# Ten attention units inside the matmul blocks of a fused kernel: one tabulated slot for every step, and B's copy on Scalar

## The chip, the cores and the metric

The kernel runs on one core of one Trainium2 chip. Its engines are PE (TensorE, the matmuls; its weight loads are shown as PEld), DVE (VectorE), ACT or Scalar (ScalarE), POOL (GpSimd) and SP (SyncE, which here only issues DMAs). Each engine works through its own queue of instructions in order and waits on semaphores for the others. The metric is the device time of one execution in microseconds (us), smaller is better; the median of three runs is 579.62 us.

## The reference, cut to what matters

Three layers follow each other; only the first mixes tokens.

```python
# x (4, 8, 768, 32), a (4, 8, 768), B and C (4, 8, 768, 16); chunks along the sequence
log_a = np.log(np.clip(a, 1e-06, 1.0))
for c in range(nc):                                  # a linear recurrence, chunk by chunk
    cum = np.cumsum(la, axis=-1)
    L = np.exp(cum[..., :, None] - cum[..., None, :]) * causal
    y_intra = (C B^T * L) @ x                        # inside the chunk
    y_inter = (C @ state) * np.exp(cum)[..., None]   # from the state before
    state = np.exp(sum(la)) * state + sum_j B_j x_j exp(cum_last - cum_j)
# y as 3072 tokens x 256 features
h = ((y @ w1) * (y @ w2)) @ w3                       # 256 -> 1024 -> 1024
x2 = h @ w_out                                       # 1024 -> 256
out = np.maximum(x2 @ w_in, 0) ** 2 @ w_out2         # 256 -> 2048 -> 256
```

## The kernel before, in words

**Blocks.** The 3072 tokens are cut into seven blocks f, four of 384 tokens and three of 512 (`FBS`). A block has a first stage of 8 steps m (`ph_a`): `a_mm` makes y @ w1 and y @ w2 for 128 of the 1024 columns, Scalar copies one result out of PSUM (`asb`), DVE multiplies (`pr`), Scalar and DVE split the product into a high and a low part (`s3h`, `s3l`), and three steps later `ff_x2` multiplies with w3 @ w_out, which is made once. Then Scalar and DVE split the 256 sums (`x2h`, `x2l`). The second stage has 16 steps (`ph_h`): `ff_h1` (6 matmuls), relu on Scalar (`r`), the square on POOL (`q`), Scalar's high part `s3h` and DVE's low part `s3l`, and, three steps later (`LAG`), `ff_o` (6 matmuls). Every product is taken as three matmuls, high x high, low x high, high x low (`mm3`, L195), for precision. For the first three steps of the second stage there is no `ff_o` yet, so these slots are short on PE (3 matmuls each, after 9 that go ahead of them). The last three `ff_o` of a block (`o_tail`) run in the first two slots of the next block; at block 4 they all run in its first slot, where the pool of 384-token tiles is replaced by one of 512 (`widen`).

**Units.** The attention layer is 16 units u: a pair of units (2j, 2j+1) is the two halves of the features of 384 tokens. The steps of one unit are:

- `u_decay` (DVE, four scans, L357): the running products of the decays, from `la`, loaded by DMA;
- `u_lw` (DVE, one short product, L369) and `u_bt` (L259): a copy of B from `bs`, loaded by DMA, to `bt`, on POOL;
- `u_bd` and `u_w2` (POOL, L375 and L386): B and the state's factors with the decays;
- `u_turn` (PE): `u_cb` (C with B, 32 small matmuls into `ub`, L445), `u_gain` (what the chunk adds to the state, L396) and, for the unit before, `u_y` (L464);
- `u_x` (Scalar) and `u_xl` (DVE): the outcome of the unit before, split into `xt` or `big`, which the first stage of a block reads; `u_loads`, the DMAs of the next unit on SP (`la`, `xa`, and for an even unit four parts each of C and B);
- `u_state` (DVE, four steps, L410), four masks `u_m` (DVE, L456: `ub` times the decays), `u_carry` (Scalar, four copies, L421).

`ub` is one PSUM tile, so a turn waits until the masks of the unit before are done.

**What sets the order.** Units 0 to 5 and blocks 0 and 1 are issued by a list of numbers (`ORDER`, run by `Plan`). From block 2 on the order is that of the code: each step m of a block is a slot, counted from 0 at block 2 (block 2: first stage 0 to 7, second 8 to 23; block 3: 24 to 31 and 32 to 47; block 4: 48 to 55 and 56 to 71; block 5: 72 to 79 and 80 to 95; block 6 from 96). In each slot `run_fill` issues what `place` has put there, behind the slot's `s3h` and in front of its `s3l`, and in front of its `ff_x2` or `ff_o`. The table `TURN` says where: before, a row of seven numbers for a unit, the slots of its six first pieces (four scans; `u_lw` with `u_bt`; `u_bd` with `u_w2`) and of its turn, while the eight pieces from the turn on stand at fixed distances of 0, 0, 1, 1, 2, 2, 3 and 3 slots behind it. The names in the order below are the program's: `la<-la,cs` a scan, `la<-ub,la` a mask, `st` a state step, `la<-la` the short product, `xtl` and `big` the outcome.

Of the kernel before, what the change touches and what calls it, by code (L numbers as in the profile page):

```python
# [102 lines left out]


TURN = {
# [4 lines left out]
}  # L110


# [26 lines left out]
def mixer_kernel(ctx, tc, a, bct, xb, cst, *rest):  # L139
# [117 lines left out]
    def u_bt(u, eng="POOL"):  # L257
        copy = nc.scalar.copy if eng == "ACT" else on[eng].tensor_copy
        copy(bt[u % 2][:, :, 0:T], bs[:, u % 2, :].rearrange("p (c i) -> p c i", i=T))  # L259
# [91 lines left out]
    def u_decay(u, h):  # L351

        if h == 0 and u >= ROWS:
            un[u] = raw[u]
        la = un[u]["la"][:, h * LH:(h + 1) * LH]
        src = rows.pop((u, h))[0:TA, :] if u < ROWS else la
        nc.vector.tensor_tensor_scan(la[:, 0:TB], src[:, 0:TB], cs, 0.0, ALU.mult, ALU.add)  # L357
        if u < ROWS:
            nc.vector.tensor_tensor(
                la[:, TB:], src[:, TB:LH],  # L360
                la[:, 0:TB].rearrange("p (c i) -> p c i", i=T)[:, :, T - 1], op=ALU.mult,
            )

    def u_lw(u):

        la = un[u]["la"].rearrange("p (h i) -> p h i", i=LH)
        if u >= ROWS:
            last = la[:, :, 0:TB].rearrange("p h (c i) -> p h c i", i=T)[:, :, :, T - 1]
            nc.vector.tensor_tensor(la[:, :, TB:], la[:, :, TB:], last, op=ALU.mult)  # L369

    def u_bd(u):

        d = un[u]
        lw = d["la"].rearrange("p (h i) -> p h i", i=LH)[:, :, TB:]
        nc.gpsimd.tensor_tensor(  # L375
            bd[u % 2][:, 0:HC * N].rearrange("p (h c n) -> p h c n", h=HG, n=N),
            d["xa"][0:T, HC * D:].rearrange("p (h c n) -> p h c n", h=HG, n=N),
            lw[0:T].unsqueeze(3).to_broadcast([T, HG, NCH, N]),
            op=ALU.mult,
        )  # L380

    def u_w2(u, eng="POOL"):
        lw = un[u]["la"].rearrange("p (h i) -> p h i", i=LH)[:, :, TB:]
        copy = nc.scalar.copy if eng == "ACT" else on[eng].tensor_copy
        for h in range(HG):
            copy(w2s[u % 2][32 * h:32 * h + N, :], lw[T:TA, h, :])  # L386
# [16 lines left out]
    def u_state(u):  # L403

        d = un[u]
        s = st[u % 2]
        c0 = NCH * ((u // 2) % 2)
        g = d.get("g") or [d["yu"][:, TB + c * D:TB + (c + 1) * D] for c in range(NCH)]
        for c in range(NCH):
            nc.vector.scalar_tensor_tensor(  # L410
                s[:, c0 + c + 1, :], s[:, c0 + c, :], w2s[u % 2][:, c:c + 1],
                g[c], ALU.mult, ALU.add,
            )

    def u_carry(u):

        d = un[u]
        s = st[u % 2]
        c0 = NCH * ((u // 2) % 2)
        for h in range(HG):  # L420
            nc.scalar.copy(  # L421
                d["xa"][T:TA, h * NCH * D:(h + 1) * NCH * D].rearrange("p (c d) -> p c d", d=D),
                s[32 * h:32 * h + N, c0:c0 + NCH, :],
            )
# [27 lines left out]
    def u_m(u, h):  # L452

        d = un[u]
        s = d["la"][:, h * LH:h * LH + TB]
        nc.vector.tensor_tensor(s, d.pop(("cb", h))[0:TA, :], s, op=ALU.mult)  # L456
# [14 lines left out]
    def u_x(u):  # L471

        d = un[u]
        d["x"] = []
        j, g = divmod(u, 2)
        i0 = 0
        while i0 < TB:
            f = max(f for f in range(NF) if F0[f] <= j * TB + i0)
            i1 = min(F0[f] + FBS[f] - j * TB, TB)
            if i0 % T or i1 - i0 < T:  # L480
                i1 = min(i1, i0 - i0 % T + T)
                src = d["y"][:, i0 // T, i0 % T:i0 % T + i1 - i0]
            else:
                i1 -= i1 % T
                src = d["y"][:, i0 // T:i1 // T, :]
            if f not in xt:
                if f < WIDE:
                    xt[f] = [sb.tile([128, KD, FB], F32R, tag=f"xt{p}", name=f"xt{p}", bufs=2) for p in "hl"]
                else:
                    if f == WIDE:  # L490
                        big.append(late.tile([128, NRL, KD, FBL], F32R, tag="rawl", name="big"))
                    xt[f] = [big[0][:, 2 * (f % 2) + i] for i in range(2)]
            at0 = j * TB + i0 - F0[f]
            hi, lo = (t[:, g, at0:at0 + i1 - i0] for t in xt[f])
            if len(src.shape) == 3:
                hi, lo = (t.rearrange("p (c i) -> p c i", i=T) for t in (hi, lo))
            nc.scalar.copy(hi, src)
            d["x"].append((lo, src, hi))
            i0 = i1

    def u_xl(u):
        raw.pop(u)
        for lo, src, hi in un.pop(u)["x"]:
            nc.vector.tensor_tensor(lo, src, f32(hi), op=ALU.subtract)

    def u_loads(u):
        if EARLY + 2 <= u < NU:
            load_la(u)
            load_xa(u)
            if u % 2 == 0:  # L510
                for h in range(HG):
                    load_ct(u // 2, h)
                    load_bt(u // 2, h)

    def u_turn(u):
        if u < NU:
            u_cb(u)
            u_gain(u)
        if u > EARLY:
            u_y(u - 1)  # L520

    def u_first(u):
        return [
            *(lambda h=h: u_decay(u, h) for h in range(HG)),
            lambda: (u_lw(u), u_bt(u)),
            lambda: (u_bd(u), u_w2(u)),
        ]

    def u_then(u):
        steps = [  # L530
            lambda: u_turn(u),
            lambda: (u > EARLY and u_x(u - 1), u_loads(u + 1)),
            lambda: u > EARLY and u_xl(u - 1),
            lambda: u_state(u),
            lambda: u_m(u, 2),
            lambda: u_m(u, 3),
            lambda: (u_carry(u), u_m(u, 0)),
            lambda: u_m(u, 1),
        ]
        return steps if u < NU else steps[:3]  # L540
# [294 lines left out]
    def place(i, f):  # L835
        fill.setdefault(PLANNED * (M1 + M2) + i, []).append(f)

    for u in range(EARLY, NU + 1):
        if u < NU:
            for i, f in zip(TURN[u], u_first(u)):  # L840
                place(i, f)
        for i, f in zip((0, 0, 1, 1, 2, 2, 3, 3), u_then(u)):
            place(TURN[u][-1] + i, f)

    def ph_a(f, tail):
        for m in range(M1):
# [126 lines left out]
```

## Time and profile before

| | |
|---|---|
| median of 3 runs | 579.62 us (578.86 to 580.37) |
| profiled execution: its own time, and its span | 579.46 us, 577.5 us |
| PE / PEld busy | 559.3 us (97%) / 492.9 us (85%) |
| DVE / Scalar / POOL busy | 335.8 (58%) / 280.7 (49%) / 140.4 us (24%) |
| chain that ended last | PE 87%, DMA 4%, DVE 3%, Scalar 2% |
| HBM read and written | 39.55 MB and 3.25 MB |

The span goes from the first to the last instruction; the execution's own time has the start and the end around it. The loads of weights fill the first 100 us; from 190 us on, where block 2 and the table begin, the core moves little data. PE is the engine that is nearly always busy. Its busy time is that of modelled ends: matmuls are pipelined, and one is shown for longer than the distance to the next. So the time that PE loses is read from its waits and from the distance of starts, not from the busy share.

### The profile page before, as it was taken

The numbers are of one execution on the slowest core, as the hardware profiler recorded it, in microseconds if no ns is written. First come the engines' busy times: TensorE is split into PE (matmuls) and PEld (weight loads), VectorE is DVE, ScalarE is ACT, GpSimd is POOL, SyncE is SP. The second block draws the span as 40 slices with busy tenths as digits, with TensorE's granted clock in tenths as the row PEclk, the third lists the DMA queues.
The fourth block names the chain that finished last, engine by engine and source line by source line (L and its number), as shares of the span: only waits on it lengthen the run. The fifth ranks groups of instructions, "written<-read, shape, count | busy, mean of one in ns | idle before, by whom it ended". The sixth has DMA issues, their size and how long they took to land.

```text
span 577.5 us, 10665 instructions
## 1 busy us (share of the span) xinstructions
PE 559.3 (97%) x4182; PEld 492.9 (85%) x4182; DVE 335.8 (58%) x603; ACT 280.7 (49%) x571; POOL 140.4 (24%) x194
## 2 busy tenths in 40 slices
PE   7898999999999999999989999999999999999997
PEld 5777999999999988999979978788888778888885
DVE  6789899993655555774687454394244532232421
ACT  3678778853455334543354342454432454333543
POOL 3133223010000104641145400353200533000532
PEclk8899999999999998999999999999999999999999
DMA  7998958100120002124203200122000000000000
GB/s 230 380 330 276 294 186 211 43 1 28 53 83 19 28 1 72 25 71 116 57 22 97 71 28 0 49 49 70 1 37 1 1 1 1 36 1 0 1 1 38
DMA packets 16891, 43.49 MB, mean 75 GB/s; under 512 B 2712, under 2 KB 6024, under 8 KB 16840
## 3 DMA queue, kind: packets, MB, share of 16 engines
q1 hardware_dynamic: 16552, 42.58, 24.1%
q8 instruction: 33, 0.54, 0.4%
q10 hardware_dynamic: 288, 0.22, 0.2%
q14 instruction: 18, 0.15, 0.1%
HBM read 39.55 MB, written 3.25 MB: 74 GB/s over the span
## 4 chain that ended last, share of the span: by engine, by line
PE 87%; DMA 4%; DVE 3%; ACT 2%; issue 1%; POOL 1%; SPq 0%; POOLq 0%; ACTq 0%; DVEq 0%
PE pw L195 44%; PE acc L195 34%; PE acc L658 3%; DMA rawe<-in_w3t 3%; DMA rawl<-in_wo 2%; PE ub L445 1%; PE ub L464 1%; DVE la L357 1%; PE ub L396 1%; PE yu L464 1%; PE pacc L195 1%; ACT r L612 1%; PE cb L445 1%; ACT xa L421 0%; DVE pr L570 0%
## 5 line engine op out<-in xcount | busy, mean ns | idle before, releaser
L620 POOL TENSOR_TENSOR q<-r 128x512 f32<-128x512 f32 (+1 forms) x81 | 85.0, 1052 | 248.9 <-ACT r L612 219.8
L627 DVE TENSOR_TENSOR s3l<-q,s3h 128x384 fp32r<-128x384 f32 (+1 forms) x112 | 75.8, 686 | 101.3 <-POOL q L620 90.9
L195 PE MATMUL acc<-s3h,wo 128*128 128x384 f32 (+1 forms) x448 | 126.4, 363 | 0.0
L612 ACT ACTIVATE r<-pw 128x384 f32<-128x384 f32 (+1 forms) x107 | 56.9, 534 | 95.1 <-PE pw L195 89.5
L195 PEld LDWEIGHTS acc<-s3h,wo 128*128 128x128 f32 x448 | 82.6, 189 | 9.1 <-issue 0.3
L195 PE MATMUL acc<-s3l,wo 128*128 128x384 f32 (+1 forms) x224 | 81.2, 363 | 1.0 <-DVE s3l L627 1.0
L570 DVE TENSOR_TENSOR pr<-pw,asb 128x384 f32<-128x384 f32 (+1 forms) x56 | 34.3, 613 | 74.4 <-PE pw L195 67.4
L195 PE MATMUL pw<-x2l,wih 128*128 128x384 f32 (+1 forms) x214 | 76.8, 363 | 0.0
L624 ACT ACTIVATE s3h<-r 128x384 fp32r<-128x384 f32 (+1 forms) x112 | 63.7, 570 | 10.8 <-PE acc L195 7.7
L580 ACT CAST s3h<-pr 128x512 fp32r<-128x512 f32 (+1 forms) x47 | 26.7, 569 | 65.3 <-DVE pr L570 61.7
L566 ACT COPY asb<-pw 128x384 f32<-128x384 f32 (+1 forms) x56 | 29.3, 525 | 50.2 <-PE pw L195 42.4
L357 DVE TENSOR_TENSOR_SCAN la<-la,cs 112x384 f32<-112x384 f32 x48 | 53.2, 1138 | 0.0
L195 PEld LDWEIGHTS acc<-s3l,wo 128*128 128x128 f32 x224 | 42.3, 189 | 5.4 <-DVE s3l L627 1.3
L195 PEld LDWEIGHTS pw<-x2l,wih 128*128 128x128 f32 x214 | 40.3, 188 | 4.4 <-DVE x2l L599 0.2
L195 PE MATMUL pw<-x2h,wih 128*128 128x384 f32 x124 | 42.3, 341 | 0.0
L195 PE MATMUL pw<-x2h,wil 128*128 128x384 f32 x124 | 42.0, 339 | 0.0
L583 DVE TENSOR_TENSOR s3l<-pr,s3h 128x384 fp32r<-128x384 f32 (+1 forms) x52 | 32.1, 620 | 15.9 <-ACT s3h L580 15.6
L195 PE MATMUL acc<-s3l,wch 128*128 128x384 f32 (+1 forms) x104 | 37.9, 365 | 1.3 <-DVE s3l L583 1.3
L195 PE MATMUL acc<-s3h,wch 128*128 128x384 f32 (+1 forms) x104 | 38.2, 367 | 0.0
L195 PE MATMUL acc<-s3h,wcl 128*128 128x384 f32 (+1 forms) x104 | 37.8, 364 | 0.0
L195 PE MATMUL pw<-big,wih 128*128 128x512 f32 x90 | 36.0, 400 | 0.0
L658 PE MATMUL acc<-wo1v,ve 128*128 128x256 f32 x128 | 32.1, 402 | 3.8 <-DVE ve L315 2.9
(146 smaller groups left out, 1048.7 us busy)
## 6 DMA issues: line engine op xcount, KB each, us to landing
la<-az SPq DMA_DIRECT2D x12, 679.0 KB, 4.9
xa<-in_xb SPq DMA_DIRECT2D x16, 288.0 KB, 5.8
rawe<-in_w3t SPq DMA_DIRECT2D x9, 512.0 KB, 9.1
rawl<-in_wo SPq DMA_DIRECT2D x7, 512.0 KB, 7.4
rawl<-in_w3t SPq DMA_DIRECT2D x7, 512.0 KB, 9.2
rawe<-in_wo SPq DMA_DIRECT2D x5, 512.0 KB, 7.3
rawl<-in_w SPq DMA_DIRECT2D x5, 512.0 KB, 8.2
rawl<-in_w_in SPq DMA_DIRECT2D x5, 512.0 KB, 5.4
```

The source lines that it names most:

```text
L195: nc.tensor.matmul(ps, lhsT=w[i == 1], rhs=x[i == 2], start=first and i == 0, stop=last and i == 2)
L357: nc.vector.tensor_tensor_scan(la[:, 0:TB], src[:, 0:TB], cs, 0.0, ALU.mult, ALU.add)
L445: nc.tensor.matmul(d["cb", h][0:TA, c * T:(c + 1) * T], lhsT=bt[u % 2][r, c, :], rhs=d["ct"][r, c * T:(c + 1) * T], start=True, stop=True,)
L566: nc.scalar.copy(ab[m], ab.pop((m, 0)))
L570: nc.vector.tensor_tensor(pr, ab.pop((m, 1)), ab[m], op=ALU.mult)
L580: (nc.scalar.copy if eng == "ACT" else on[eng].tensor_copy)(pt[f, m][0], ab[m])
L583: nc.vector.tensor_tensor(pt[f, m][1], ab.pop(m), f32(pt[f, m][0]), op=ALU.subtract)
L612: nc.scalar.activation(hr[m], hp.pop(m), AF.Relu)
L620: on[eng].tensor_tensor(q, hr[m], hr[m], op=ALU.mult)
L624: nc.scalar.activation(qt[f, m][0], hr[m], AF.Square)
L627: nc.vector.tensor_tensor(qt[f, m][1], hr.pop((m, 0)), f32(qt[f, m][0]), op=ALU.subtract)
L658: nc.tensor.matmul(wps[f][j // 2][:, (j % 2) * DM:(j % 2 + 1) * DM], lhsT=t[:, j * 128:(j + 1) * 128], rhs=wo1v[:, k, :].bitcast(F32), sta ...
```

## The change

`TURN` has two tuples for a unit: six slots for the first pieces and eight for the pieces from the turn on, so that each has a slot of its own (for unit 16, which only finishes unit 15, three). The numbers come from a search over a small schedule. `u_bt` of these ten units is called with "ACT": B's copy runs on Scalar.

```diff
 TURN = {
-    6: (0, 0, 1, 1, 2, 2, 4), 7: (7, 7, 8, 8, 9, 9, 11), 8: (14, 14, 15, 16, 16, 17, 19),
...
+    6: ((1, 5, 5, 6, 6, 6), (8, 9, 9, 9, 9, 10, 10, 10)),
+    7: ((2, 3, 3, 4, 7, 8), (13, 13, 13, 13, 14, 14, 17, 18)),
...
     def u_first(u):
         return [
             *(lambda h=h: u_decay(u, h) for h in range(HG)),
-            lambda: (u_lw(u), u_bt(u)),
+            lambda: (u_lw(u), u_bt(u, "ACT")),
             lambda: (u_bd(u), u_w2(u)),
         ]
...
     for u in range(EARLY, NU + 1):
         if u < NU:
-            for i, f in zip(TURN[u], u_first(u)):
+            for i, f in zip(TURN[u][0], u_first(u)):
                 place(i, f)
-        for i, f in zip((0, 0, 1, 1, 2, 2, 3, 3), u_then(u)):
-            place(TURN[u][-1] + i, f)
+        for i, f in zip(TURN[u][1], u_then(u)):
+            place(i, f)
```

The turns stood in slots 4, 11, 19, 26, 31, 38, 46, 58, 66, 82 and (unit 16) 89; they stand now in 8, 13, 20, 25, 31, 39, 46, 57, 70, 80 and 93. Lines of the changed kernel from `TURN` on have numbers that are higher by 7.

DVE before, from slot 6 of block 2 to the start of its second stage (`pr` and `s3l` are the first stage's, `x2l` ends it, `s3l<-q` is the second stage's):

```order
L570 TENSOR_TENSOR pr<-pw,asb 128x384
L456 TENSOR_TENSOR la<-ub,la 112x384 x2
L583 TENSOR_TENSOR s3l<-pr,s3h 128x384
L570 TENSOR_TENSOR pr<-pw,asb 128x384
L456 TENSOR_TENSOR la<-ub,la 112x384 x2
L357 SCALAR_TENSOR_TENSOR la<-la,cs 112x384 x2
L583 TENSOR_TENSOR s3l<-pr,s3h 128x384
L599 TENSOR_TENSOR x2l<-acc,x2h 128x384 x2
L357 SCALAR_TENSOR_TENSOR la<-la,cs 112x384 x2
L627 TENSOR_TENSOR s3l<-q,s3h 128x384
```

DVE now, from slot 5 to the start of the second stage:

```order
L577 TENSOR_TENSOR pr<-pw,asb 128x384
L364 SCALAR_TENSOR_TENSOR la<-la,cs 112x384 x2
L590 TENSOR_TENSOR s3l<-pr,s3h 128x384
L577 TENSOR_TENSOR pr<-pw,asb 128x384
L364 SCALAR_TENSOR_TENSOR la<-la,cs 112x384
L376 TENSOR_TENSOR la<-la 112x4x4
L590 TENSOR_TENSOR s3l<-pr,s3h 128x384
L577 TENSOR_TENSOR pr<-pw,asb 128x384
L376 TENSOR_TENSOR la<-la 112x4x4
L590 TENSOR_TENSOR s3l<-pr,s3h 128x384
L606 TENSOR_TENSOR x2l<-acc,x2h 128x384 x2
L634 TENSOR_TENSOR s3l<-q,s3h 128x384
```

Unit 7's first two scans stood between the last `pr` and the last `s3l` of the first stage; now all eight scans of units 6 and 7 are done by slot 6, and the masks of unit 6 come in the second stage.

POOL before, the steps of units 6 to 8 (`bt`, `bd`, `w2s`) and the squares of block 2:

```order
L375 TENSOR_TENSOR bd_100<-xa,la 96x256
L386 COPY w2s_102<-la 16x4 x4
L620 TENSOR_TENSOR q<-r 128x384 x2
L259 COPY bt_107<-bs 128x4x96
L375 TENSOR_TENSOR bd_101<-xa,la 96x256
L386 COPY w2s_103<-la 16x4 x4
L620 TENSOR_TENSOR q<-r 128x384 x7
L259 COPY bt_106<-bs 128x4x96
```

Scalar now, where units 6 and 7 have their copies of B (slots 6 and 7 and the three first relus of the second stage):

```order
L266 COPY bt_106<-bs 128x4x96
L573 COPY asb<-pw 128x384
L587 CAST s3h<-pr 128x384
L266 COPY bt_107<-bs 128x4x96
L603 CAST x2h<-acc 128x384 x2
L619 ACTIVATE r<-pw 128x384
L631 ACTIVATE s3h<-r 128x384
L619 ACTIVATE r<-pw 128x384
L631 ACTIVATE s3h<-r 128x384
L619 ACTIVATE r<-pacc 128x384
```

`bt` of unit 7 stood behind two squares on POOL; now it stands on Scalar behind the last `s3h` of the first stage, five slots ahead of the turn of its unit.

DVE before, from the end of block 3's first stage (units 10 and 11):

```order
L599 TENSOR_TENSOR x2l<-acc,x2h 128x384 x2
L504 TENSOR_TENSOR big<-ub,big 128x384
L410 SCALAR_TENSOR_TENSOR st_104<-st_104,w2s_102,ub 128x32 x4
L627 TENSOR_TENSOR s3l<-q,s3h 128x384
L456 TENSOR_TENSOR la<-ub,la 112x384 x2
L627 TENSOR_TENSOR s3l<-q,s3h 128x384
L456 TENSOR_TENSOR la<-ub,la 112x384 x2
L357 SCALAR_TENSOR_TENSOR la<-la,cs 112x384 x2
L627 TENSOR_TENSOR s3l<-q,s3h 128x384
L357 SCALAR_TENSOR_TENSOR la<-la,cs 112x384 x2
L627 TENSOR_TENSOR s3l<-q,s3h 128x384
L369 TENSOR_TENSOR la<-la 112x4x4
```

DVE now, from the same place:

```order
L606 TENSOR_TENSOR x2l<-acc,x2h 128x384 x2
L364 SCALAR_TENSOR_TENSOR la<-la,cs 112x384 x2
L634 TENSOR_TENSOR s3l<-q,s3h 128x384
L417 SCALAR_TENSOR_TENSOR st_104<-st_104,w2s_102,ub 128x32 x4
L634 TENSOR_TENSOR s3l<-q,s3h 128x384 x2
L463 TENSOR_TENSOR la<-ub,la 112x384
L364 SCALAR_TENSOR_TENSOR la<-la,cs 112x384 x2
L376 TENSOR_TENSOR la<-la 112x4x4
L634 TENSOR_TENSOR s3l<-q,s3h 128x384
```

The four scans of unit 11 stood two and two behind the four masks of unit 10; now two stand in front of the first `s3l` of the second stage and two behind the first mask, and the other three masks follow them.

## Rows read from the trace of the kernel before

**Rows 1.** The page: engines' busy time; PE's granted clock in 40 slices

```profile
PE 559.3 (97%) x4182; PEld 492.9 (85%) x4182; DVE 335.8 (58%) x603; ACT 280.7 (49%) x571; POOL 140.4 (24%) x194
...
PEclk8899999999999998999999999999999999999999
```

**Rows 2.** Who PE waited for from 190 us on: us in total, times, longest

```profile
PE ub L445 <- POOL bt L259: 2.3, 2, 1.2
PE acc L195 <- DVE s3l L583: 1.3, 1, 1.3
PE pw L195 <- ACT asb L566: 1.2, 2, 0.7
PE acc L195 <- DVE s3l L627: 1.0, 1, 1.0
PE pw L195 <- DVE pr L570: 0.4, 2, 0.3
```

**Rows 3.** PE in time, end of block 2's first stage: start, us, what

```profile
216.70 0.44 PE L195 MATMUL acc<-s3l,wch 128*128 128x384 f32 x1 [1.34 <-DVE s3l L583]
216.99 0.34 PE L195 MATMUL acc<-s3h,wch 128*128 128x384 f32 x1
```

**Rows 4.** The chain behind the turns of units 7 and 8: start, us

```profile
225.59 0.91 PE ub L464 x32
226.50 2.22 PE acc L195 x6
228.72 1.41 PE pw L195 x6
...
246.32 0.70 PE ub L464 x32
247.03 1.24 PE acc L195 x6
248.27 1.06 PE pw L195 x6
```

**Rows 5.** Behind unit 7's turn: busy time by engine, PEclk, DMA

```profile
226.00:229.00 3.00, 3.00 (x23) 2.72 (x13) 2.15 (x4) 0.48 (x1) 1.60 (x2) 0.50 0.53 177
```

**Rows 6.** DVE in order of time, slot 7 of block 2

```profile
214.40 1.80 DVE L357 TENSOR_TENSOR_SCAN la<-la,cs 112x384 f32<-112x384 f32 x2
```

**Rows 7.** B's copy by engine: duration in ns, least/median/most

```profile
L259 POOL COPY bt<-bs x15: 498/505/1681, 7.6 to 411.1; 128x384 f32<-128x384 f32 x15
...
L259 ACT COPY bt<-bs x1: 511/511/511, 7.6 to 7.6; 128x384 f32<-128x384 f32 x1
```

**Rows 8.** POOL in order of time, ahead of unit 11's turn

```profile
301.02 1.68 POOL L259 COPY bt<-bs 128x384 f32<-128x384 f32 x1
```

**Rows 9.** SP's DMA issues behind unit 11's turn, first and last: start, us

```profile
304.98 0.31 SPq L235 DMA_DIRECT2D la<-az  x1
...
313.01 0.31 SPq L255 DMA_DIRECT2D bs<-in_bct  x1
```

**Rows 10.** Time to landing of the DMAs into la, then of those into bs

```profile
DMA to landing us min/median/max: 4.4/4.9/6.3
...
DMA to landing us min/median/max: 1.8/5.1/6.2
```

**Rows 11.** Scalar in order of time, block 4's second slot

```profile
338.60 1.22 ACT L421 COPY xa<-st 16x128 f32<-16x128 f32 x4
```

**Rows 12.** DVE's groups by form from 225 us on: xcount, busy us, mean ns

```profile
L357 DVE TENSOR_TENSOR_SCAN la<-la,cs 112x384 f32<-112x384 f32 x32 | 37.2, 1188 | 0.0
...
L456 DVE TENSOR_TENSOR la<-ub,la 112x384 f32<-112x384 f32 x36 | 18.3, 549 | 0.0
...
L410 DVE SCALAR_TENSOR_TENSOR st<-st,w2s,ub 128x32 f32<-128x32 f32 x36 | 8.8, 245 | 1.0
```

**Rows 13.** The page's groups of the square and the low part

```profile
L620 POOL TENSOR_TENSOR q<-r 128x512 f32<-128x512 f32 (+1 forms) x81 | 85.0, 1052 | 248.9 <-ACT r L612 219.8
L627 DVE TENSOR_TENSOR s3l<-q,s3h 128x384 fp32r<-128x384 f32 (+1 forms) x112 | 75.8, 686 | 101.3 <-POOL q L620 90.9
```

12 rows, old and new, of the table TURN are left out of this document.

## The prediction

> **What bounds the kernel now.** I read the page first, then PE's waits, then the places of these waits in time. The page has PE busy for 97% of the span [rows 1], so only what makes PE wait, or slows it, can move the end. From 190 us on, where the tabulated units begin, PE's waits are few [rows 2]: 2.3 us in two waits for B's copy on POOL (`bt`), 1.3 and 1.0 us for `s3l` of DVE, 0.4 us in two pieces for `pr` of DVE, and 1.2 us in two pieces for `asb` of Scalar. All are within two slots of a step of a unit. Nothing else there is idle on PE, and the matmuls themselves are the same before and after, so the change can give back these waits, what hangs on them, and no more.
>
> A wait costs more than its row says. Matmuls are shown longer than their spacing: one takes 0.34 us at 216.99 [rows 3], while six of them pass in 1.06 us [rows 4], 0.18 us apart, so each idle time starts 0.16 us late in the rows.
>
> The Trainium skill says the same in general (Trainium Kernel Development and Optimization, Performance Expectations): busy time of the matmul row is a bad measure, since matmuls are pipelined. By the idle column alone the waits below would be 5.5 us; by the spacing they are 6.6 us, and the trace is on the side of the page.
>
> One wait has a second price. After PE waited for unit 7's `bt` its granted clock is 0.50, the 1.2 GHz level, from 226 to 229 us [rows 5]. The same work after the turns of unit 7 and unit 8 [rows 4] takes 0.91 against 0.70, 2.22 against 1.24 and 1.41 against 1.06 us: 0.2 + 1.0 + 0.35 = 1.5 us lost. Behind the other turns the page's clock line stays at its highest digit [rows 1].
>
> **The change, part by part.** PE's instructions are the same in number; ten groups of them (a unit's turn) stand elsewhere. Nothing before slot 0 of block 2 (about 189 us) moves.
>
> *Scans away from the last slot of a first stage.* Before, unit 7's first two scans stand at 214.40 between `pr` and `s3l` of slot 7 [rows 6], 1.80 us, and PE, which needs this `s3l` at once, waits 1.34 us at 216.70 [rows 3]. In the new order only a short product stands there, while DVE would wait for Scalar's `s3h` anyway: that wait (1.3) goes. The two 0.4 us pieces for `pr` come from two scans in each of slots 0 and 1; now slot 0 has none and slots 1 and 2 have one each: they go. The 1.0 us for `s3l` is unit 11's four scans in slots 34 and 35, right behind unit 10's masks; now they are in 32 and 35, with the state and masks spread over 33 to 36: it goes, with little to spare (below).
>
> *B's copy to Scalar.* On POOL it takes 0.50 us alone [rows 7] but 1.68 at 301.02, beside DVE's scans [rows 8], and stands behind squares in the order; both `bt` waits of PE (2.3) are this. On Scalar the one row there is takes 0.51 us [rows 7]. Ten copies are 5.1 us on an engine that is busy for 49% of the span, and they stand two to seven slots ahead of their turns, so none is on the path. The bounds of one copy are 0.5 and, if Scalar suffered as POOL did, 1.7 us; even that is less than a slot (12 x 0.18 = 2.1 us in the second stage), of which, at 49% busy, Scalar's own operations take about half. I take 0.5, hidden. POOL keeps the `bd` and `w2` steps and its squares, which loses it nothing.
> The copy adds a wait to Scalar: for B's load. SP starts a pair's loads when the turn ends; before, it issued unit 12's decays at 304.98 and the last B part at 313.01 [rows 9], which lands at least 1.8 us later [rows 10], so 9.8 us after the turn. In the new table unit 12's copy stands four slots behind its load; eight sixes of matmuls (8.5 us) and Scalar's two operations of a slot (about 1 us) bring it there after 9.5 us, so it waits some 0.3 us, with the next relu behind it. PE needs that relu only when its PSUM buffer is taken again, one slot and a half later (18 matmuls, 3.2 us, of which the relu itself takes about a sixth): a wait of up to 2 us is hidden. For units 8 and 10 it is five and four slots (the four are long ones), for 14 ten.
>
> *The state's copies.* Unit 12's four copies `xa<-st` take 1.22 us on Scalar at 338.60 [rows 11], ahead of the next `asb`, in a slot of block 4 without `x2` matmuls; that is the shorter `asb` wait (1.2 - 0.7 = 0.5). They move to slot 54, a full slot: it goes. The other, 0.7 us, is at slot 48, where the wide pool replaces the narrow one and `asb` waits for the old tiles' last matmul. Nothing of that changes: it stays.
>
> *What is packed closer.* Three scans now share a slot (units 8, 12, 14), and units 9, 11, 12 and 13 scan one or two slots after their decays are loaded. A scan takes 1.19 us on average, a mask 0.55, a state step 0.25 [rows 12]. Three scans and an `s3l` (0.69 [rows 13]) are 4.3 us in a slot of 2.1, 2.2 late; `s3l` is used three slots on, 6.3 us, of which relu, the square (1.05 [rows 13]) and `s3l` itself need some 2.4, so about 4 us may be lost before PE notices. The tightest stretch is the start of block 3's second stage (slots 32 to 38). From `x2l` to unit 11's turn DVE has 4 scans (4.75), a state (1.0), 4 masks (2.2), 5 `s3l` (3.4): 11.4 us. PE has 9 + 48 + 6 matmuls of 0.177, 11.1 us, and starts some 0.5 later: 11.6. At the border of blocks 2 and 3 (slots 21 to 23) the same count leaves DVE 0.4 us ahead of PE. Decays land 4.4 to 6.3 us after issue [rows 10]; unit 12's scans, two slots behind the turn, come up after two sixes of matmuls and the 2.4 us of the chain to `s3l`, 4.1 us after the issue (0.2 of it passes before), so DVE loses 0.3 to 2.2 there, and PE, by the 4 us above and the masks in front of the turn in slot 46, nothing to 0.4. For all of this I add 0.2 us; the bounds are 0 and, if two of the tight places miss by as much as the waits of before did (1.2 each) and the clock falls once (1.5), 3.9.
>
> The output store of block 2 moves behind unit 10's ten loads on SP. Its `o` tile shares a buffer with `pr`, but in the new program only the `pr` of slot 31 waits for that store, some 17 us on; no cost.
>
> **The sum.** Idle 2.3 + 1.3 + 1.0 + 0.4 + 0.5 = 5.5; seven waits x 0.16 = 1.1; clock 1.5; less 0.2: 7.9 us. The profiled execution took 579.46, so 571.6; the median of the runs is 0.16 above it, so 571.7.
>
> **Rivals.**
> *The waits move.* DVE's work is not less, only spread otherwise, and two stretches have under 0.5 us in hand. For it: the sums of 11.4 and 11.6, and means that hide longer scans beside POOL. Against: `bt` no longer disturbs there, and alone a scan is near 0.9 (two in 1.80). Two waits of 1.2 and a fall of the clock: 571.7 + 3.9 = 575.6, spread from 573.5 to 577.5.
> *The clock falls without a wait.* The turn's narrow matmuls, not the wait, may have done it; then a fall stays somewhere: 573.2. Against: nine turns without a drop, one of them (unit 11's) behind a wait of 1.1. It lies inside the forecast's range.
> By the Trainium skill (TensorE: Matmul & The Clock Gate, Why this matters for your kernels) the fall belongs to idle gaps longer than any in these rows; by that rule the 1.5 would not hang on the wait, as in this rival; the one fall in the trace stands behind the longest wait but one.
> *The change does not do what it says.* Scalar's copy, in order behind relu, `s3h` and a load, is as late as POOL's was, and the turns wait as before; with the spread scans 3 us are won, with a late Scalar two of them are lost again behind Scalar: within 0.3%, about 578.5. Against: the copies stand two slots or more ahead.
> *Slower: scans wait for their load.* DVE is in order; a scan that waits for its decays holds up `s3l`, `pr` and the masks of the turn. Six units (8, 9, 10, 11, 12, 13) now scan about when the landing is due, 4 to 6 us after the turn. While it lands by 6.3 us, PE's share is small; from about 7.5 us on each of the six costs PE 1.4 and more, and the gain of 7.9 is gone. At 8 us it is 6 x 1.8 = 10.8: 582. For it: the loads compete with B's and C's. Against: 6.3 is the longest of eight.
>
> **How the numbers follow.** Forecast 0.62 (own range 570.5 to 573.4), waits move 0.20, the clock 0.05, not as said 0.06, slower 0.07. A run of this kernel tells 0.3% (1.7 us) from no change, so faster means under 577.9: 0.62 + 0.20 + 0.05 = 0.87; same 0.06; slower 0.07. The range leaves out 0.15 at the top; below 569.9 there would have to be a gain besides the waits.
>
> **What would show it.** No PE wait for `bt` in the waits; no `s3l` wait of 1 us in slots 7 and 35; PE clock 1.00 from 190 us to the end; the wait for `asb` at slot 48 still there; Scalar idle before some `bt` for the load without a PE wait behind it. Wrong would be PE waits for masks, `s3l` or `pr` at slots 24 to 26, 35 to 39 or 46, or DVE's scans waiting more than 2 us for `la`.

## The result, and the profile after

The changed kernel took 569.38 us as a median of four runs (569.02 to 570.82), the kernel before 579.24 us in the same comparison (four runs): a ratio of 0.983, 95% interval 0.981 to 0.986. Five later runs of the changed kernel gave 569.69 beside 578.66 for before, ratio 0.984 (0.981 to 0.986). The direction and the mechanism came as predicted. The time, 571.7 predicted, was 2.3 us too high, and 569.38 lies 1.1 us below the forecast's own range (570.5 to 573.4) and 0.5 us below 569.9, under which the prediction expected nothing.

The page of the changed kernel, profiled at 569.02 us; the lines answer to [rows 1], the columns of the first are busy time, share of the span and instructions:

```profile
span 567.1 us, 10661 instructions
PE 555.2 (98%) x4182; PEld 491.4 (87%) x4182; DVE 330.1 (58%) x603; ACT 285.8 (50%) x581; POOL 134.4 (24%) x184
...
PEclk8999999999999999999999999999999999999999
```

PE's busy time fell by 4.1 us (559.3 to 555.2) while the span fell by 10.4. The busy share, 97% before and 98% now, says next to nothing of that.

All that PE waited for from 186 us to the end (columns: engine, output and line, releaser; us in total, times, longest), where before there were five groups [rows 2]:

```profile
PE pw L202 <- ACT asb L573: 0.7, 1, 0.7
```

Only the `asb` wait of slot 48 is left, the one that the prediction said would stay. No new wait came in its place. The clock behind unit 7's turn, now from 222.8 to 225.1 us, in stretches of the changed kernel (columns: stretch, its length, busy time of PE, PEld, DVE, ACT and POOL with instructions, then granted clock, DMA share, GB/s), beside 0.50 in [rows 5]:

```profile
222.00:226.00 4.00, 4.00 (x108) 3.51 (x107) 1.74 (x4) 2.04 (x5) 2.11 (x2) 1.00 0.02 4
226.00:232.00 6.00, 6.00 (x36) 6.00 (x35) 4.99 (x11) 2.20 (x5) 2.26 (x2) 1.00 0.97 215
```

And the chain behind that turn (start, length, matmuls), to be read beside [rows 4]:

```profile
224.47 0.70 PE ub L471 x32
225.17 1.27 PE acc L202 x6
226.44 1.06 PE pw L202 x6
227.50 1.06 PE acc L202 x6
```

The sixes that took 2.22 and 1.41 us behind the wait of before are at 1.27 and 1.06 now. B's copy, by engine and form (shortest, median and longest in ns), and what the queue of Scalar did just ahead of it:

```profile
L266 ACT COPY bt<-bs x10: 495/502/515, 206.8 to 417.2; 128x384 f32<-128x384 f32 x10
L266 ACTq EVENT_SEMAPHORE  x9: 17/17/38, 206.4 to 386.6; - x9
```

All ten take 0.50 us, where POOL's went up to 1.68 [rows 7], and none waits for B's load: the 0.3 us that the prediction gave to unit 12's copy did not come.

DVE now waits for decays, which it never did from block 2 on before. The total, and the longest of the four in its place (DVE's timeline; idle time and releaser in brackets):

```profile
DVE la L364 <- DMA la<-az: 5.2, 4, 3.2
```

```profile
315.63 0.75 DVE L511 TENSOR_TENSOR big<-ub,big 128x96 fp32r<-128x96 f32 x4 [0.42 <-ACT big L504]
319.56 0.96 DVE L364 TENSOR_TENSOR_SCAN la<-la,cs 112x384 f32<-112x384 f32 x1 [3.17 <-DMA la<-az]
320.43 0.53 DVE L634 TENSOR_TENSOR s3l<-q,s3h 128x384 fp32r<-128x384 f32 x1
```

That is unit 13's scan in slot 47. DVE stands for 3.2 us, `s3l` behind it stands late with it, and PE has no wait there, since it uses this `s3l` only in the next block's first slot.

**Where the time went.** The start of each block can be read from PE's first matmul of it. From block 2's start to the last instruction the profiles show 388.45 us before (189.09 to 577.54) and 379.48 after (187.60 to 567.08): 8.97 less, of which 5.35 in block 2, 2.35 in block 3, 1.00 in block 4, 0.26 in block 5. Another 1.49 us lies ahead of block 2, where both run the same program.

### The profile page after: what moved, and what is told of

It reads as the page before. It is cut to its first block, busy times and chain, and to the rows that moved or that the text cites. A ratio compares the mean times of both kernels' runs of the same rounds, so it can differ in the third digit from the quotient of the medians.

```text
span 567.1 us, 10661 instructions
## 1 busy us (share of the span) xinstructions
PE 555.2 (98%) x4182; PEld 491.4 (87%) x4182; DVE 330.1 (58%) x603; ACT 285.8 (50%) x581; POOL 134.4 (24%) x184
## 4 chain that ended last, share of the span: by engine, by line
PE 92%; DMA 4%; DVE 2%; ACT 1%; issue 0%; ACTq 0%; SPq 0%
PE pw L202 47%; PE acc L202 36%; PE acc L665 2%; DMA rawe<-in_w3t 2%; PE ub L452 2%; DMA rawl<-in_w3t 2%; PE ub L471 1%; PE pacc L202 1%; PE acc L712 1%; PE cb L452 1%; PE ub L403 1%; DVE la L364 1%; PE yu L471 1%; DMA cs<-in_cst 1%; PE rows L351 0%
## 5 line engine op out<-in xcount | busy, mean ns | idle before, releaser
L634 DVE TENSOR_TENSOR s3l<-q,s3h 128x384 fp32r<-128x384 f32 (+1 forms) x112 | 73.1, 662 | 91.0 <-POOL q L627 80.8
L631 ACT ACTIVATE s3h<-r 128x384 fp32r<-128x384 f32 (+1 forms) x112 | 63.7, 570 | 10.8 <-PE acc L202 7.7
L382 POOL TENSOR_TENSOR bd<-xa,la 96x256 f32<-96x256 f32 x16 | 12.5, 783 | 180.5 <-DVE la L376 171.0
L364 DVE TENSOR_TENSOR_SCAN la<-la,cs 112x384 f32<-112x384 f32 x48 | 50.4, 1081 | 5.2 <-DMA la<-az 5.2
```

The lines of the kernel that those rows point to most:

```text
L382: nc.gpsimd.tensor_tensor(bd[u % 2][:, 0:HC * N].rearrange("p (h c n) -> p h c n", h=HG, n=N), d["xa"][0:T, HC * D:].rearrange("p (h c n) ...
L631: nc.scalar.activation(qt[f, m][0], hr[m], AF.Square)
L634: nc.vector.tensor_tensor(qt[f, m][1], hr.pop((m, 0)), f32(qt[f, m][0]), op=ALU.subtract)
```

## The experiments

In all diffs the kernel named is the base. "To the end" is the time from block 2's first matmul to the last instruction, in the profiled execution.

**The kernel before once more** (no edit).

> The kernel before, unchanged, to see what comes and goes without any change. Theory: the profiled run of before had a fall of PE's clock to 1.2 GHz in its first 40 us that the run of the changed kernel had not; block 2 then began at 189.1 instead of 187.6 us, though no instruction ahead of it is moved. If that is chance, the runs here show mean clocks of both kinds, 0.991 and about 0.994, times 1 to 2 us apart, and a median within 0.3% of before. Rival: the early 1.5 us belongs to the change; then every run of before has it (0.991, block 2 at 189.1).

It took 578.22 us (576.83 to 579.22, 12 runs), ratio 0.9995 (0.998 to 1.001). Its profile has the same five groups of waits, the clock at 0.86 from 220 to 232 us as in the first profile, and 388.57 us to the end (388.45 in the first). The mean clocks of its 12 runs lie between 0.991 and 1.000, so not every run of before has the early 1.5 us of the rival. The part that the table orders repeats within 0.2 us, while the runs of one program lie up to 4.6 us apart (576.1 to 580.7 over 48 runs of before).

**Scalar's copy alone**, in the kernel before:

```diff
-            lambda: (u_lw(u), u_bt(u)),
+            lambda: (u_lw(u), u_bt(u, "ACT")),
```

> The old table, with B's copy of the ten later units on Scalar. Theory: both waits of PE for that copy go (2.3 and 2 x 0.16), the fall of the clock behind the first one with them (1.5 to 1.7), and the two waits of 0.2 for bd in front of units 13 and 15, since POOL has less in front of it: 4.1 to 4.7 us faster, block 2 to the end 388.5 to 384 us. The waits for s3l (1.3 and 1.0), pr (0.4) and asb (0.7 and 0.5) stay. Rival (the turn's narrow matmuls make the clock fall): the clock is at 1.2 GHz for about 3.4 us behind unit 7's turn without a wait, gain 2.6 to 3. Rival (Scalar is as late as POOL was): waits for bt of 1 us stay, no gain.

577.02 us (575.68 to 579.23, 12 runs), ratio 0.997 (0.995 to 0.998): faster by 1.8 us, well under what was expected. PE's waits from 186 us on:

```profile
PE pw L195 <- ACT asb L566: 1.6, 3, 0.7
PE acc L195 <- DVE s3l L583: 1.3, 1, 1.3
PE ub L396 <- POOL bd L375: 1.2, 2, 0.8
PE acc L195 <- DVE s3l L627: 1.0, 1, 1.0
PE ub L445 <- ACT bt L259: 0.4, 1, 0.4
PE pw L195 <- DVE pr L570: 0.4, 2, 0.3
```

The 2.3 us of `bt` on POOL are gone and 1.2 us of `bd` stand in their place, in the same two turns, with 0.4 of `bt` on Scalar and 0.4 more for `asb`. `bd` was behind `bt` in POOL's order, and it has a second thing to wait for, the short product on DVE. POOL at units 7 and 11 (start, length; idle time and releaser in brackets):

```profile
222.95 0.89 POOL L375 TENSOR_TENSOR bd<-xa,la 96x256 f32<-96x256 f32 x1 [0.18 <-DVE la L369]
...
300.53 0.81 POOL L375 TENSOR_TENSOR bd<-xa,la 96x256 f32<-96x256 f32 x1 [1.49 <-DVE la L369]
```

At unit 11 that product (300.22 us) stood behind scans that ran until 299.85 and an `s3l`; at unit 7 (222.01 us) it stood behind an `s3l` that had waited for a square. B's copy itself reads no scan; on Scalar unit 7's stood behind two relus and two `s3h`. So unit 7's turn went only from 3.82 us (0.2 of it the lower clock) to 3.27, unit 11's from 3.50 to 3.21, against 2.33 without a wait. The 0.2 of `bd` at units 13 and 15, which were to go, stayed. The clock did not fall in this profile (1.00 from 220 us on), which is most of the 1.8.

**The table alone**, in the kernel after:

```diff
-            lambda: (u_lw(u), u_bt(u, "ACT")),
+            lambda: (u_lw(u), u_bt(u)),
```

> The new table, with B's copy on POOL as before. Theory: the waits for bt came from the place behind squares, two slots ahead of the turn, and the new table has the copy four to ten slots ahead; so nearly all of the gain stays: block 2 to the end 379.5 to 380.5 us against 388.5 before and 379.5 with the whole change. Rival: the copy has to leave POOL; one or two waits for bt of about 1.2 us come back, with or without a fall of the clock, 381 to 384 us.

569.89 us (569.19 to 570.4, 5 runs), ratio 0.985 (0.983 to 0.987); 379.73 us to the end, 0.25 more than in the first profile of after. PE's one wait is the `asb` of 0.7, every turn takes 2.33 to 2.39 us, and DVE's waits for `la` came to 7.8 us at no cost. Of the change's two parts the table does all that can be measured. The copy stands two to six slots ahead of its turn in the new table, not four to ten as expected, but at units 7 and 11, where PE had waited, it is six and four where it was two: POOL's copies start at 209.84 and 290.83 us there, and PE's turns need them at 223.50 and 296.36. What Scalar takes over is hidden either way.

**Scans still earlier**, in the kernel after, all four of a unit in one slot (units 8 to 13; two of the six rows):

```diff
-    9: ((22, 22, 23, 23, 23, 24), (25, 25, 25, 25, 25, 26, 27, 30)),
+    9: ((21, 21, 21, 21, 23, 24), (25, 25, 25, 25, 25, 26, 27, 30)),
...
-    12: ((41, 41, 41, 42, 43, 43), (46, 46, 47, 49, 51, 51, 54, 56)),
+    12: ((40, 40, 40, 40, 43, 43), (46, 46, 47, 49, 51, 51, 54, 56)),
```

> The changed kernel, with all four scans of units 8 to 13 in the first slot behind their turn (unit 11 and 13: in the one they have). DVE then waits for the decays to land, which the prediction priced as the way to a slower kernel. In the changed kernel DVE waits 5.2 us for them in four places, and PE not at all. By the forecast's slack (4 us in a slot of the second stage, 1.5 in the first) DVE's waits grow to 10 to 14 us and PE pays 0 to 3, most of it in block 3's first stage. By the rival each unit costs PE 1.4 or more: 6 to 9 us slower than the changed kernel, with falls of the clock.

580.17 us (576.61 to 584.1, 12 runs), ratio to before 1.003 (1.001 to 1.005), 10.6 us above the changed kernel's median of nine runs (569.58). PE's waits, and DVE's for the load:

```profile
PE acc L202 <- DVE s3l L634: 3.7, 3, 2.4
PE pw L202 <- DVE pr L577: 3.5, 1, 3.5
PE pw L202 <- ACT asb L573: 0.7, 1, 0.7
```

```profile
DVE la L364 <- DMA la<-az: 12.4, 6, 3.9
```

Behind each of the two longest waits the clock fell. PE's timeline at the first, and the stretches around both:

```profile
233.93 0.52 PE L202 MATMUL acc<-s3h,wo 128*128 128x384 f32 x2
236.81 0.68 PE L202 MATMUL acc<-s3l,wo 128*128 128x384 f32 x1 [2.36 <-DVE s3l L634]
```

```profile
236.00:240.00 4.00, 3.19 (x10) 3.19 (x11) 3.28 (x7) 0.46 (x2) 1.79 (x2) 0.61 0.01 2
...
274.00:278.00 4.00, 4.00 (x15) 3.99 (x15) 1.88 (x4) 2.46 (x7) 0.00 (x0) 0.57 0.00 0
```

Idle 7.2 more, four waits x 0.27 (the price of a wait between wide matmuls, worked out below), and two falls of 1.5 are 11.3; the profile needs 390.94 us to the end, 11.5 more than the first of after, and the medians are 10.6 apart. Both expected sizes (0 to 3, and 6 to 9) were too small. The direction is that of the prediction's slower rival: what stands in front of `s3l` and `pr` on DVE holds them. But the edit does two things at once, it starts the scans before their load has landed and it puts four of them in one piece. DVE ahead of the longest wait:

```profile
269.10 3.50 DVE L364 TENSOR_TENSOR_SCAN la<-la,cs 112x384 f32<-112x384 f32 x4 [1.95 <-DMA la<-az]
```

Here the load took 1.95 us of DVE and the piece of four scans 3.50, while in the changed kernel 3.2 us for a load with one scan behind it cost PE nothing. No run separates the two.

**The last wait**, in the kernel after, at block 4's first slot:

```diff
+            stores = []
...
-            stores = []
+                if f == WIDE and m == i == 0:
+                    while tail:
+                        stores += tail.pop(0)(False) or []
...
-                while tail:
-                    stores += tail.pop(0)(False) or []
```

The first line stands ahead of the slot's loop over i, and the new block inside that loop, behind `a_mm(f, m, i)`; the two lines taken away at the end stood behind the loop.

> The kernel after, but at block 4's first slot (48) the three last ff_o of block 3 stand between the two a_mm of that slot (w1's, then the 18 matmuls of ff_o, then w2's), no longer behind both. The one wait of PE that the new order left, 0.7 us for asb, stands there because the wide asb waits for the narrow pool's last readers. My theory (only waits are left to win on PE, and one is worth its idle time and 0.16): the wait goes, 0.85 us less than the kernel after, so about 568.6. Rival (the wait only moves: pr or s3h of the slot are late instead, or w2's matmuls wait for a bank): within 0.3 us of the kernel after, and the waits list shows another releaser of 0.5 us or more in that slot.

568.94 us (568.33 to 569.41, 4 runs), ratio to before 0.982 (0.980 to 0.984). The list of PE's waits from 186 us on is empty. It needs 378.96 us to the end, 0.5 and 1.0 less than two profiles of after, and the median is 0.75 below that of after in the same comparison (569.69); the runs overlap (568.33 to 569.41 against 568.78 to 572.0), so the profile carries this more than the times do. Its median is the lowest here.

**The kernel after once more** (no edit).

> The kernel after once more, to size the miss. My theory: from block 2's start to the end it takes 379.5 us against 388.4 before, 9.0 less (8.5 to 9.5), of which the prediction counted 7.9; what lies ahead of block 2 is the same program and differs by up to 1.5 us from execution to execution, with the number of falls of the clock in it. So 569.2 to 570.3 as a median, and 8.7 to 9.5 less than before. Rival (the first four executions were lucky): 571 or more, less than 8.3 below before. A second rival (there is a gain ahead of block 2 too, from the other place of the code): its block 2 starts 1 us or more ahead of before's again, in an execution with the same falls of the clock.

569.69 us (568.78 to 572.0, 5 runs), 8.97 below before in the same comparison, and 379.99 us to the end, 8.5 less than before. That is the size that the first rival denied. PE's waits:

```profile
PE pw L202 <- ACT asb L573: 0.7, 1, 0.7
PE acc L202 <- DVE s3l L634: 0.2, 1, 0.2
```

Block 2 began at 190.11 us here, the latest of ten profiles (187.60, in the first of after, is the earliest). So nothing is won ahead of block 2, and the 1.49 us there were scatter.

**Three entries of the new table**, in the kernel before (its entries written as two tuples):

```diff
-    7: ((7, 7, 8, 8, 9, 9), (11, 11, 12, 12, 13, 13, 14, 14)),
+    7: ((2, 3, 3, 4, 7, 8), (11, 11, 12, 12, 13, 13, 14, 14)),
...
-    10: ((28, 28, 29, 29, 29, 30), (31, 31, 32, 32, 33, 33, 34, 34)),
-    11: ((34, 34, 35, 35, 36, 36), (38, 38, 39, 39, 40, 40, 41, 41)),
+    10: ((28, 28, 29, 29, 29, 30), (31, 31, 31, 33, 35, 36, 36, 36)),
+    11: ((32, 32, 35, 35, 35, 36), (39, 39, 39, 40, 40, 42, 44, 44)),
```

> The kernel before, with only three entries of the table replaced by the new ones: unit 7's six first pieces (scans in slots 2, 3, 3, 4 in place of 7, 7, 8, 8; its turn stays in slot 11), unit 10's pieces from its turn on, and unit 11's whole entry. B's copies stay on POOL. My theory (the gain sits in two places): unit 7's bt wait of 1.2 and s3l wait of 1.3 go and the fall of the clock with them (1.5), unit 11's bt wait of 1.1 and s3l wait of 1.0 go, four waits x 0.16: 6.7 us, so about 572.1 where before is at 578.8; left are pr 0.4, asb 1.2 and 0.2 each for bd at units 13 and 15. Rival (the search's gain is in all ten units together, and single entries put in by hand disturb their neighbours): 4 us or less, over 574.8, with new waits of PE of 1 us or more beside these entries.

572.18 us (570.81 to 572.95, 4 runs), ratio 0.988 (0.986 to 0.990): 6.5 of the 9.0 us (6.9 in the profile: 381.56 to the end). PE's waits:

```profile
PE pw L202 <- ACT asb L573: 1.2, 2, 0.7
PE pw L202 <- DVE pr L577: 0.4, 2, 0.3
```

The two `bt` and the two `s3l` waits are gone, those that were left alone stand as in [rows 2], nothing new came, and the clock is 1.00 from 220 us on. Two places hold most of the gain.

**A late bd**, in the kernel after: the sixth piece of units 7, 8, 12 and 14 in the slot of their turn (one of the four rows):

```diff
-    7: ((2, 3, 3, 4, 7, 8), (13, 13, 13, 13, 14, 14, 17, 18)),
+    7: ((2, 3, 3, 4, 7, 13), (13, 13, 13, 13, 14, 14, 17, 18)),
```

> The kernel after, but the sixth piece (bd and w2s on POOL) of units 7, 8, 12 and 14 stands in the slot of the unit's own turn, behind that slot's square on POOL. So PE has to wait in four turns for bd, behind narrow matmuls: relu 0.5, square 1.05 and bd 0.8 from the slot's last ff_h1 matmul on, less the turn's first 1.0: 1.2 to 2.0 us each, 4.8 to 8 together, and 0.16 more each. The question is the clock. My theory (the fall of the clock to the 1.2 GHz level at unit 7's turn before hung on PE's wait there): one to four of these four turns have a fall right behind the wait, each 1.5 us more, so 5.5 to 14 us above the kernel after, and more than the idle times and 0.16 each. Rival (the fall came and went by itself, as those in the first 50 us): no fall behind any of the four waits; the time is above the kernel after by the idle times and 0.16 each, 5.4 to 8.6 us, and nothing beyond.

577.57 us (575.32 to 580.16, 10 runs), 8.0 above the nine runs of after. PE's waits, and the stretches around unit 7's turn:

```profile
PE ub L403 <- POOL bd L382: 5.0, 4, 1.5
PE pw L202 <- ACT asb L573: 0.7, 1, 0.7
```

```profile
224.00:228.00 4.00, 2.85 (x100) 2.53 (x100) 0.65 (x2) 1.49 (x3) 2.39 (x7) 0.94 0.01 4
228.00:232.00 4.00, 4.00 (x17) 4.00 (x16) 2.77 (x8) 0.67 (x2) 0.08 (x1) 0.63 0.87 252
232.00:236.00 4.00, 4.00 (x25) 4.00 (x24) 1.79 (x3) 1.85 (x4) 1.58 (x2) 1.00 0.54 80
```

With a wait of 1.2 us put back into unit 7's turn the clock falls behind it again. Behind the other three, 1.2 to 1.5 us long, it does not fall in this profile. The four turns are 1.22, 1.22, 1.26 and 1.54 us longer, 5.24 in all; with one fall of 1.5 that is near the 7.0 by which the profile is longer to the end (386.43 us), and the rest of the 8.0 between the medians fits more falls in other runs. The mean granted clock of the ten runs is 0.9929, which times a span of 575 leaves 4.1 us of work undone, against 1.6 us in the 18 runs of the changed kernel, its repetition, the table alone and the last wait (0.9971 of 568): 2.5 more.

## Why the prediction was right in its mechanism and wrong in its size

The prediction's losses, measured again in the trace of before as the distance between starts of matmuls less the usual one (0.175 us for 384 columns, 0.23 for 512), the matmul behind a wait included, and turns against 2.33 and 2.39 us:

| | counted | measured |
|---|---|---|
| `pr`, slots 0 and 1, two waits | 0.72 | 0.95 |
| `s3l`, slot 7 | 1.46 | 1.62 |
| unit 7's turn | 1.36 | 1.28 |
| clock behind it, its last 0.2 us in the turn included | 1.5 | 1.53 |
| `s3l`, slot 35 | 1.16 | 1.27 |
| unit 11's turn | 1.26 | 1.17 |
| `asb`, unit 12's state | 0.66 | 0.81 |
| `bd` in the turns of units 13 and 15 | 0 | 0.41 |
| sum | 8.1 | 9.0 |
| packed DVE | -0.2 | 0 |
| sum, and block 2 to the end | 7.9 | 8.97 |

The mechanism held: every wait that was to go is gone, with the fall of the clock, and three entries of the table won 6.5 us where the expectation had 6.7. Three steps of the sum had the wrong size, 1.1 us together, and its start was 0.9 too high.

**The first step that failed: "seven waits x 0.16 = 1.1".** The seven waits cost some 1.5 us more than their idle time. The 0.16 is right ahead of a wait, but the matmul behind a wait is late too. [rows 3] has it: from the first matmul behind the wait to the next it is 0.29 us (216.70 to 216.99), and from there on 0.17:

```profile
216.99 0.34 PE L195 MATMUL acc<-s3h,wch 128*128 128x384 f32 x1
217.16 0.34 PE L195 MATMUL acc<-s3h,wcl 128*128 128x384 f32 x1
```

These 0.11 us stand behind all five waits between wide matmuls, which so cost their idle time and 0.27. The two waits in front of a turn cost only 0.07 and 0.08 more than their idle time. So the prediction had 0.16 for all, where 0.27 and 0.08 were measured.

**The second: "Nothing else there is idle on PE".** It was read from PE's matmul row alone. The weight loads have waits of their own, in the trace of before and, on the last line, of the changed kernel from 186 us on:

```profile
PEld ub L396 <- POOL bd L375: 0.6, 2, 0.3
PEld ub L445 <- POOL w2s L386: 0.5, 2, 0.3
...
PEld ub L452 <- issue: 2.2, 8, 0.4
```

The two waits for `bd` are lost time: the turns of units 13 and 15 take 2.6 us, against 2.39 after. In PE's row they do not show, since the narrow matmuls ahead of them are shown longer than their spacing. The `w2s` line is no loss: the first weight load of every turn without a wait has such a gap of 0.25 or 0.37 us, in the changed kernel too, and those two turns (units 10 and 12) take the usual 2.33 us. A line of this row counts only where the turn is longer.

**The third** is the allowance of 0.2 us for packed DVE, which was for nothing.

That busy time of the matmul row is a bad measure of how near a kernel is to its limit is what the Trainium skill says (Trainium Kernel Development and Optimization, Performance Expectations). This trace agrees: 4.1 us of busy time for 10.4 of span.

Some readings of the new table were off without effect on the sum: unit 14's scans are two and two, not three in a slot; two of the ten turns (units 10 and 12) stay in their slots; and B's copies stand two to six slots ahead of their turns, not two to seven.

**The base.** Of the 2.3 us these three steps are 1.1. Of the rest 0.9 us is the start of the sum: 579.46 for the profile and 579.62 for the median of three runs, where 60 runs of the program (48 of before, 12 of its repetition) have a median of 578.7. The last 0.3 us is less than the changed kernel's own scatter: its first four runs have a median of 569.38, all nine 569.58. The prediction's low end was drawn from the terms alone ("below 569.9 there would have to be a gain besides the waits"), with no room for the scatter of a program whose runs lie up to 4.6 us apart. This scatter lies ahead of block 2 for a good part: its start moved between 187.60 and 190.11 us in ten profiles. What moves it stays open: the clock falls there in some executions and not in others, but two runs of after with a mean clock of 1.00 took 568.78 and 570.84 us.

**The clock.** The prediction tied the fall to the wait, with a rival that the narrow matmuls did it. The fall is there in both profiles of before behind a `bt` wait; it is gone in the six profiles without a wait in that turn, whose narrow matmuls are the same; it is back when the wait is. That is good evidence, in nine profiles, for the wait as a condition of the fall at this turn. It isn't sufficient: two waits of 0.4 at unit 7's turn and one of 0.8 at unit 11's (Scalar's copy alone), `bt` waits of 1.1 at unit 11's turn (both profiles of before) and three `bd` waits of 1.2 to 1.5 us (late `bd`) had none behind them, while 2.4 and 3.5 us did (scans still earlier). Why unit 7's turn has it and the others have not stays open. By the Trainium skill (TensorE: Matmul & The Clock Gate, Why this matters for your kernels) the fall belongs to idle gaps longer than the 1.2 us at unit 7's turn. This trace does not agree, and the measurement decides. As a mean over runs the term is near 1.3 us rather than 1.5: 56 runs of before and its repetition have a mean clock of 0.9949, 2.9 us of 577, against the 1.6 above.

**Scalar's copy.** It was given the 2.3 us of both `bt` waits, and ten copies of which the prediction says "I take 0.5, hidden". The cost was right. The gain was credited to the wrong part: alone it turned `bt` waits into `bd` waits, and the table alone won all that can be measured. The forecast of the whole change was not touched by that, but a sum by edits would have been.

**The rivals.** *The waits move* was wrong for this table: the stretches with under 0.5 us in hand held, and the mean scan went from 1138 to 1081 ns on the page. *Slower* had the right mechanism: DVE did wait for `la` (5.2 us here, against the 2 us that the prediction named as a sign of being wrong), at no cost to PE. That sign was chosen badly, since a wait of DVE counts only with a wait of PE behind it. With the scans up to four slots earlier and four in a piece it cost 10.6 us. That this is near the prediction's 10.8 is luck: those were six units at 1.8 us, and here it was four waits and two falls of the clock.

## What to carry to other kernels

Price a wait by the starts of the matmuls on both sides of it, read the waits of the weight loads beside the matmul row's and test them on the lengths of equal pieces, and take the base of a forecast from many runs: here these sizes, not the mechanism, made the miss. A late engine has a line behind it: moving one late operation away shows the next one in that line, so find what the whole line waits for, here also the short product on DVE. Work may stand ahead of its load only as far as its engine has time in hand, since an engine in order passes each wait, and each long piece, on to all that stands behind it.

## What the runs showed of the hardware

- Behind a wait of PE between wide matmuls the first matmul started 0.29 us ahead of the next where 0.175 is usual (384 columns), at all four such waits in the trace of before. Two waits of 0.3 us of the weight loads for `bd` cost 0.2 us each, with no wait in the matmul row.
- Four waits of 1.2 to 1.5 us, each in a turn of 96 narrow matmuls (late `bd`): TensorE's clock fell to its 1.2 GHz level behind one of them, the same turn as before. Behind waits of 2.4 and 3.5 us between wide matmuls (scans still earlier) it fell both times.
- The same copy of 128x384 elements took 0.50 us in all ten places on Scalar, and 0.50 to 1.68 us on POOL, where the long one began beside DVE's scans.
